# A fused attention and two-layer mixture kernel in two token passes, with Strassen's products in the first layer too

## The chip, the cores and the metric

The kernel runs on one core of a Trainium2 chip. The metric is the device time of one execution in microseconds (us). The core's engines are TensorE (PE, with its weight loads as PEld), VectorE (DVE), ScalarE (ACT), GpSimd (POOL) and SyncE (SP), which issues the DMAs.

## The reference: what is computed

Attention within chunks of 64 tokens (4 batches, 8 heads, 576 tokens, head size 64) gives x of 2304 tokens x 512. Layer 1 is a gated product, layer 2 a mixture of four experts:

```python
scores = (q_c @ k_c.T) / sqrt(64); attn = softmax(scores); x = (attn @ v_c) as (2304, 512)
x = ((x @ w_a) * (x @ w_b)) @ w_out                # w_a, w_b: 512 x 1536, float64; w_out: 1536 x 512
p = domain_probs / (domain_probs.sum(-1) + 1e-9)   # 2304 x 4
out = sum over e of p[:, e] * (relu(x @ w1[e]) @ w2[e])   # w1: 512 x 1024, w2: 1024 x 512
```

## The kernel before

Tokens lie in 18 tiles of 128, grouped in five blocks: block 0 has two tiles, blocks 1 to 4 have four (512 columns in a matmul). Every float32 operand of a large product is split in a high part in fp32r (a cast on ACT, `split_hi`, L90) and a low part (a subtraction on GpSimd or VectorE), and a product is three matmuls: high x low, high x high, low x high (`mm3`, `half_mm`).

The order of the work is written out by hand: lists of small steps (closures) are called one after the other, and each engine runs what it is given in that order. There is one DMA queue, SP's.

**Start.** q, k and v of a tile are loaded (k into a tile `kbd` with zeros beside it, so that two heads are one product), then `emit_S` (scores, PE), `emit_A` (maximum and subtraction, DVE, L218 and L220), `emit_exp` (ACT), `emit_B` (sum and reciprocal on DVE, product on GpSimd, L235), `emit_T` (transposition on PE, copy on ACT) and `emit_V` (PE; ACT casts the high part of x, DVE subtracts the low part, L282). After four tiles, `attn_slot` does one stage of each for successive tiles, between the matmuls of layer 1's first f chunk.

**Layer 1** goes over 12 f chunks of 128, and for each over all five blocks: `moe1_steps` makes the products with w_a and w_b (4 x 3 matmuls each), ACT copies the first, DVE multiplies by the second (L348), the result is split (L90, L352), and one block later `x2_steps` multiplies by w_out (4 x 3 matmuls) and DVE adds into the accumulator `xacc` (L382). Weights come as 512 KB of float64 per piece; `from_f64` turns the two words into float32 with four instructions on DVE (L126 to L132), one on ACT and an integer addition on GpSimd (L142), and `split_w` splits the piece (low part on GpSimd, L149).

**End of layer 1.** `combos` forms, from the accumulators of blocks 1 and 2, the quarter sums of Strassen's algorithm in Winograd's form (B11, B21, T1 to T4, B22), each split (L408, L411).

**Layer 2** goes twice over 16 g (pairs of f chunks of the experts): the first pass p = 0 has blocks 1, 2 and 0, the second blocks 3 and 4. `w_steps` prepares a g: the weights' sums S1 to S4 on GpSimd and six splits. `emit_h_pair` makes the hidden layer of two blocks with 7 products of half depth (6 matmuls each) instead of 8, `emit_h0` block 0's plainly, and `o_tiles` multiplies by w2 and adds p times the result into `oacc` (L582). PSUM is one pool of eight 2 KB buffers.

## Time and profile before

| | |
|---|---|
| median of 3 runs | 1275.64 us (1275.56 to 1276.01) |
| profiled execution, its own time | 1275.81 us |
| its span, first to last instruction | 1273.8 us |
| TensorE busy | 1253.6 us (98%), 6626 instructions |
| VectorE busy | 731.5 us (57%) |
| GpSimd busy | 550.9 us (43%) |
| ScalarE busy | 378.2 us (30%) |
| DMA | 72.43 MB |

Busy shares are means over the span; TensorE's matmuls overlap in the records, so a busy TensorE is not one at its peak. The time outside the span is 2.0 us.

### The profile page before, as it was taken

How to read it: one execution, taken by the hardware profiler on the slowest of the kernel's cores; microseconds unless marked ns; L12 is line 12 of the kernel's file. 1: busy time of each engine (PE TensorE's matmuls, PEld its weight loads, DVE VectorE, ACT ScalarE, POOL GpSimd, SP SyncE). 2: the span in 40 equal slices, each digit the busy share in tenths (PEclk: the TensorE clock that was granted, in tenths of full speed). 3: DMA queues.
4: the chain of work that ended last, by engine and by line, in shares of the span. 5: the costliest groups of instructions: out<-in, count | busy, mean ns of one | idle time of the engine just before them, and what ended most of it. 6: DMA issues, size and time to landing. Idle time of an engine off the chain costs nothing.

```text
span 1273.8 us, 16939 instructions
## 1 busy us (share of the span) xinstructions
PE 1253.6 (98%) x6626; PEld 1048.0 (82%) x6628; DVE 731.5 (57%) x1161; ACT 378.2 (30%) x675; POOL 550.9 (43%) x493
## 2 busy tenths in 40 slices
PE   7899999999999999899999999999999999999998
PEld 5788888888888888688888888888888888888887
DVE  7863555565555555656566555555565556555555
ACT  3554222222222222432332222322232332333231
POOL 4432334343333435455444434344345455554542
PEclk9999999999999999899999999999999999999999
DMA  8731111111111110011110111111131111111111
GB/s 275 223 102 29 38 34 50 50 50 34 49 34 33 50 50 1 33 34 36 48 50 34 34 50 39 45 34 50 33 133 40 60 50 50 51 49 66 34 50 67
DMA packets 25279, 72.43 MB, mean 57 GB/s; under 512 B 3184, under 2 KB 3184, under 8 KB 25200
## 3 DMA queue, kind: packets, MB, share of 16 engines
q1 hardware_dynamic: 25200, 71.35, 17.7%
q8 instruction: 52, 0.85, 0.3%
q14 instruction: 27, 0.22, 0.1%
HBM read 66.62 MB, written 4.72 MB: 56 GB/s over the span
## 4 chain that ended last, share of the span: by engine, by line
PE 92%; DVE 5%; POOL 1%; issue 1%; ACT 1%; DMA 0%; SPq 0%; DVEq 0%; POOLq 0%
PE ps L595 31%; PE ps L479 24%; PE ps L318 12%; PE ps L319 12%; PE ps L320 12%; PE ps L269 1%; DVE d L220 1%; DVE sm L231 1%; DVE mx L218 1%; DVE xl L282 0%; DVE cv L126 0%; DVE sm L232 0%; PE ps L204 0%; POOL cB L408 0%; DMA kbd<-in_k_dram 0%
## 5 line engine op out<-in xcount | busy, mean ns | idle before, releaser
L149 POOL TENSOR_TENSOR wl<-raw,wh 128x512 fp32r<-128x512 f32 x128 | 166.3, 1299 | 340.0 <-ACT wh L90 340.0
L582 DVE SCALAR_TENSOR_TENSOR oacc<-ps,pr,oacc 128x512 f32<-128x512 f32 x270 | 192.5, 750 | 141.4 <-PE ps L595 141.4
L595 PE MATMUL ps<-wl,hh 128*128 128x512 f32 x576 | 224.3, 389 | 0.0
L595 PE MATMUL ps<-wh,hh 128*128 128x512 f32 x576 | 224.2, 389 | 0.0
L595 PE MATMUL ps<-wh,hl 128*128 128x512 f32 x576 | 224.1, 389 | 0.0
L318 PE MATMUL ps<-xl,wh 128*128 128x512 f32 (+1 forms) x488 | 179.7, 368 | 2.3 <-DVE xl L282 1.8
L319 PE MATMUL ps<-xh,wh 128*128 128x512 f32 (+1 forms) x488 | 178.1, 365 | 0.0
L320 PE MATMUL ps<-xh,wl 128*128 128x512 f32 (+1 forms) x488 | 178.0, 365 | 0.0
L479 PE MATMUL ps<-cT,wh 128*128 128x512 f32 x512 | 157.6, 389 | 0.0
L348 DVE TENSOR_TENSOR asb<-ps,asb 128x512 f32<-128x512 f32 (+1 forms) x61 | 38.4, 630 | 191.4 <-PE ps L320 158.5
L352 POOL TENSOR_TENSOR gl<-asb,gh 128x512 fp32r<-128x512 f32 (+1 forms) x61 | 73.2, 1200 | 171.9 <-ACT gh L90 171.9
L382 DVE TENSOR_TENSOR xacc<-ps,xacc 128x512 f32<-128x512 f32 (+1 forms) x220 | 132.3, 633 | 4.0 <-PE ps L320 4.0
L595 PEld LDWEIGHTS ps<-wh,hl 128*128 128x128 f32 x576 | 108.1, 188 | 22.6
L595 PEld LDWEIGHTS ps<-wl,hh 128*128 128x128 f32 x576 | 108.2, 188 | 22.1
L595 PEld LDWEIGHTS ps<-wh,hh 128*128 128x128 f32 x576 | 108.2, 188 | 21.8
L479 PE MATMUL ps<-cB,wh 128*128 128x512 f32 x384 | 118.2, 389 | 0.0
L479 PEld LDWEIGHTS ps<-cT,wh 128*128 128x128 f32 x512 | 96.1, 188 | 20.0
L318 PEld LDWEIGHTS ps<-xl,wh 128*128 128x128 f32 x488 | 92.0, 188 | 18.5 <-DVE xl L282 2.6
L320 PEld LDWEIGHTS ps<-xh,wl 128*128 128x128 f32 x488 | 92.0, 188 | 14.9
L319 PEld LDWEIGHTS ps<-xh,wh 128*128 128x128 f32 x488 | 92.1, 189 | 14.4
L149 POOL TENSOR_TENSOR wl<-s,wh 128x512 fp32r<-128x512 f32 x64 | 83.2, 1299 | 47.2 <-ACT wh L90 47.2
L479 PE MATMUL ps<-cT,wl 128*128 128x512 f32 x256 | 99.6, 389 | 0.0
(85 smaller groups left out, 1962.6 us busy)
## 6 DMA issues: line engine op xcount, KB each, us to landing
raw<-in_w2p_dram SPq DMA_DIRECT2D x64, 512.0 KB, 3.5
raw<-in_w1p_dram SPq DMA_DIRECT2D x36, 512.0 KB, 3.6
q<-in_q_dram SPq DMA_DIRECT2D x18, 256.0 KB, 4.7
kbd<-in_k_dram SPq DMA_DIRECT2D x36, 128.0 KB, 5.2
v<-in_v_dram SPq DMA_DIRECT2D x18, 256.0 KB, 3.3
out_dram<-oacc SPq DMA_DIRECT2D x18, 256.0 KB, 2.0
pr<-in_probs_dram SPq DMA_DIRECT2D x1, 36.0 KB, 5.2
```

The costliest lines, as they stand in the source:

```text
L149: nc.gpsimd.tensor_tensor(out=lo, in0=r, in1=hi.bitcast(F32), op=ALU.subtract)
L218: nc.vector.tensor_reduce(out=mx, in_=ps, axis=AX.X, op=ALU.max)
L220: nc.vector.tensor_tensor(out=d, in0=ps, in1=mx.to_broadcast([P, H, CH]), op=ALU.subtract)
L318: nc.tensor.matmul(out=ps[:, :n], lhsT=wh, rhs=al, start=(m == 0), stop=False)
L319: nc.tensor.matmul(out=ps[:, :n], lhsT=wh, rhs=ah, start=False, stop=False)
L320: nc.tensor.matmul(out=ps[:, :n], lhsT=wl, rhs=ah, start=False, stop=(m == last))
L348: nc.vector.tensor_tensor(out=g[:, :n], in0=st[1][:, :n], in1=g[:, :n], op=ALU.mult)
L352: nc.gpsimd.tensor_tensor(out=gl[:, :n], in0=g[:, :n], in1=gh[:, :n].bitcast(F32), op=ALU.subtract)
L382: nc.vector.tensor_tensor(out=ac, in0=ps[:, :n], in1=ac, op=ALU.add)
L479: nc.tensor.matmul(out=ps, lhsT=x, rhs=y, start=first and kk == 0 and m == 0, stop=kk == 1 and m == 2, skip_group_check=not first,)
L582: nc.vector.scalar_tensor_tensor(out=o, in0=ps, scalar=p1, in1=o, op0=ALU.mult, op1=ALU.add)
L595: nc.tensor.matmul(out=ps[k], lhsT=x[:, s], rhs=y, start=f == 0 and m == 0, stop=f == 1 and m == 2,)
```

## The change

Layer 1 too is done in two token passes, the first over blocks 0, 1 and 2, the second over 3 and 4. Its f chunks are taken in six pairs F. Pair 0 is plain in the first pass (in the attention's place); pairs 1 to 5 of the first pass and all six of the second make the products of two blocks with w_a and w_b by the seven half-depth products that layer 2 already used (`seq`, `seq_a`, `seq_b`); block 0 stays plain (`block0`). `x2_steps` adds both chunks of a pair in one PSUM group. Attention of tiles 13 to 17 moves into the first pass's pairs 1 to 4.

The first pass writes each prepared weight tile (high and low part, 128 x 1024 float32) to DRAM (`entry`, `save`); the second reads it back (`fetch`), and one ACT copy makes it fp32r. The pieces of pair 0 are converted again at the end of the second pass. Layer 2 does the same between its passes. The weights' sums are on DVE (`w_sums`). `from_f64` works in place in the loaded tile. The keys lose their zeros: `emit_S` has 16 products over 64 rows in two PSUM buffers, and `emit_A` four instructions for two. PSUM is two pools of four buffers. The sums over blocks 1 and 2 for layer 2 are formed within the second pass of layer 1, its subtractions on GpSimd.

```diff
+    w_p = ctx.enter_context(tc.tile_pool(name="w", bufs=8))
...
+    ps_p = ctx.enter_context(tc.tile_pool(name="ps", bufs=4, space=bass.MemoryType.PSUM))
+    psm_p = ctx.enter_context(tc.tile_pool(name="psm", bufs=4, space=bass.MemoryType.PSUM))
...
+    def save(behind=0):
+        while len(unsaved) > behind:
+            key, t = unsaved.pop(0)
+            saved[key] = tc.dram_tile([P, 2, 512], F32, name="kept" + "_".join(map(str, key)))
+            nc.sync.dma_start(out=saved[key], in_=t.bitcast(F32))
...
+    def fetch():
+        key = to_fetch.pop(0)
+        save()
...
+        nc.sync.dma_start(out=r, in_=saved[key])
+        fetched[key] = r
...
+    def entry(w, key, names, src, keep):
+        if src is None:
+            t = w_tile()
+            nc.scalar.copy(out=t, in_=fetched.pop(key))
+            if to_fetch and to_fetch[0][0] == key[0]:
+                fetch()
+        else:
+            t = split_w(src)
+            if keep:
+                unsaved.append((key, t))
+                save(2)
...
+    def w_sums(a11, a12, a21, a22):
...
+        add(s1, a21, a22)
+        add(s3, a11, a21, ALU.subtract)
+        add(s2, s1, a11, ALU.subtract)
+        add(s4, a12, s2, ALU.subtract)
...
+    def conv(F, i):
+        key = (0, 2 * F + i % 2, i // 2)
+        f32s[F, i] = from_f64(raws[key].pop(0))
...
+    def seq(w, t, on):
...
+        pa = psum_m()
+        half_mm(pa, w("A11"), c["B11"])
+        nc.scalar.copy(out=t["m1"], in_=pa)
+        yield
+        pb = psum_m()
+        half_mm(pb, w("S2"), c["T2"])
+        add(t["u2"], pb, t["m1"])
+        yield
+        half_mm(pa, w("A12"), c["B21"], first=False)
+        out("11", pa)
+        yield
...
+    def seq_b(F):
...
+        def on(name, ap):
+            g = ga[name]
+            add(g, ap, g, ALU.mult)
+            gh[name], gl[name] = gh_tile(name), ag_tile(F32R)
+            to_parts(g, gh[name], gl[name])
...
+    def x2_steps(F, j, first, last):
...
+            ws = [tuple(x[:, s] for x in wts[0, F][f]) for f in range(2)]
+            mm3(ps, [(*ws[f], *gp[f]) for f in range(2)], n)
...
+        for F in range(1, NP1):
...
+            units = steps_of(seq_a(F, t), 7) + [lambda f=f: block0(F, 0, f) for f in range(2)]
+            units += steps_of(seq_b(F), 7) + [lambda f=f: block0(F, 1, f) for f in range(2)]
...
+            x2p = x2_steps(F, 1, False, last) + x2_steps(F, 2, False, last)
...
+            units += x2p + [lambda i=i: (x20[i](), x20[i + 1]()) for i in (0, 2)]
...
+            put(1, lambda: ent(F, 5, True))
+            put(2, lambda: conv(F, 4))
+            put(3, lambda: ent(F, 6, True))
+            put(5, lambda: (ent(F, 7, True), load_w()))
+            put(6, lambda: conv(F, 5))
...
+                put(10, lambda: conv(nF, 0))
+                put(12, lambda: ent(nF, 0, True))
+                put(14, lambda: conv(nF, 1))
+                put(17, lambda: (sums(nF, 0), load_w()))
+                put(18, lambda: conv(nF, 2))
...
+        order = (*range(1, NP1), 0)
...
+            sa = steps_of(seq_a(F, t), 7)
+            units = sa[:2] + x2
+            units += [lambda: (temps(), sa[2]())] + sa[3:] + steps_of(seq_b(F), 7)
```

`put(u, go)` lets `go` be called ahead of unit u; `conv` and `ent` call `from_f64` and `entry` for piece i or entry n of a pair, `sums` calls `w_sums`.

## Rows read from the trace of the kernel before

**Rows 1.** The page: the share of the chain that ended last by engine, and the busy time and instructions of each engine:

```profile
PE 1253.6 (98%) x6626; PEld 1048.0 (82%) x6628; DVE 731.5 (57%) x1161; ACT 378.2 (30%) x675; POOL 550.9 (43%) x493
...
PE 92%; DVE 5%; POOL 1%; issue 1%; ACT 1%; DMA 0%; SPq 0%; DVEq 0%; POOLq 0%
```

**Rows 2.** Busy time of each engine in two stretches, layer 1 after the attention and the end of layer 1: the stretch and its length, busy us and instructions by engine, granted clock, share of the DMA engines, GB/s:

```profile
101.30:484.00 382.70, 382.70 (x1856) 323.94 (x1857) 207.70 (x367) 95.48 (x172) 138.23 (x111) 1.00 0.14 42
516.70:530.20 13.50, 8.33 (x38) 7.14 (x38) 10.72 (x14) 4.26 (x6) 5.17 (x4) 0.75 0.12 39
```

**Rows 3.** The chain that ended last in order of time, pieces of layer 2: start us, length us, what. L479 is the hidden products of two blocks, L595 those with w2; between a piece of L479 and the next of L595 lie block 0's 24 matmuls of 256 columns, off the chain:

```profile
565.78 13.63 PE ps L595 x60
579.40 9.52 PE ps L479 x42
591.80 13.63 PE ps L595 x60
...
953.20 10.88 PE ps L595 x48
```

**Rows 4.** The timeline of TensorE at the end of layer 1: start us, recorded duration us, engine, line, shapes, count, and in brackets the idle time before and what ended it. 24 matmuls of 256 columns start from the first row up to the second; 12 of 512 columns from the fourth up to the fifth:

```profile
495.88 0.28 PE L318 MATMUL ps<-xl,wh 128*128 128x256 f32 x1
...
498.75 0.40 PE L318 MATMUL ps<-gl,wh 128*128 128x512 f32 x1
...
516.34 0.39 PE L320 MATMUL ps<-gh,wl 128*128 128x512 f32 x1
521.90 0.79 PE L318 MATMUL ps<-gl,wh 128*128 128x512 f32 x1 [5.17 <-POOL gl L352]
...
527.18 0.30 PE L318 MATMUL ps<-yl,wh 128*128 128x256 f32 x1
```

**Rows 5.** The timeline of TensorE in the attention, one slot (scores, transposition, attention x v, layer 1), and the first 512-column chunk:

```profile
31.41 1.09 PE L204 MATMUL ps<-kbd,q 128*64 128x128 f32 x16
32.44 0.66 PE L241 MATMUL ps<-ident,d 128*128 128x128 f32 x4
33.02 1.15 PE L269 MATMUL ps<-aT,v 64*64 64x64 f32 x32
34.10 0.39 PE L318 MATMUL ps<-xl,wh 128*128 128x256 f32 x1
...
72.31 0.50 PE L318 MATMUL ps<-xl,wh 128*128 128x512 f32 x1
```

**Rows 6.** The timeline of VectorE in an attention slot (sum of exponentials, low half of x, maximum, subtraction, first instruction of a conversion):

```profile
42.97 0.69 DVE L231 TENSOR_REDUCE sm<-d 128x8 f32<-128x512 f32 x1 [0.37 <-ACT d L225]
...
44.02 0.64 DVE L282 TENSOR_TENSOR xl<-ps,xh 128x512 fp32r<-128x512 f32 x1
44.57 0.68 DVE L218 TENSOR_REDUCE mx<-ps 128x8 f32<-128x512 f32 x1
45.36 0.69 DVE L220 TENSOR_TENSOR d<-ps,mx 128x512 f32<-128x512 f32 x1
45.96 1.31 DVE L126 TENSOR_SCALAR cv<-raw 128x512 f32<-128x512 f32 x1
```

**Rows 7.** The timeline of VectorE at the end of layer 1: subtractions of two SBUF operands, 1024 wide:

```profile
504.01 2.19 DVE L411 TENSOR_TENSOR xacc<-xacc,xacc 128x1024 f32<-128x1024 f32 x1
506.24 1.65 DVE L411 TENSOR_TENSOR xacc<-xacc 128x1024 f32<-128x1024 f32 x1
...
517.76 1.21 DVE L411 TENSOR_TENSOR xacc<-xacc,xacc 128x1024 f32<-128x1024 f32 x1
```

**Rows 8.** The timeline of GpSimd at the same places (the attention's product; low halves of the sums and of a product):

```profile
45.95 1.05 POOL L235 TENSOR_TENSOR d<-d,rc 128x512 f32<-128x512 f32 x1
...
500.35 4.78 POOL L408 TENSOR_TENSOR cB<-xacc,cB 128x1024 fp32r<-128x1024 f32 x2
505.08 1.72 POOL L352 TENSOR_TENSOR gl<-asb,gh 128x256 fp32r<-128x256 f32 x1
```

**Rows 9.** The timeline of VectorE in the middle of layer 1: four additions from PSUM of 512 columns, the four instructions of a conversion, four additions of 256 columns:

```profile
202.71 2.48 DVE L382 TENSOR_TENSOR xacc<-ps,xacc 128x512 f32<-128x512 f32 x4
205.10 0.42 DVE L126 TENSOR_SCALAR cv<-raw 128x512 f32<-128x512 f32 x1
205.55 0.43 DVE L129 TENSOR_SCALAR cv<-cv 128x512 f32<-128x512 f32 x1
205.89 0.42 DVE L131 TENSOR_SCALAR sg<-raw 128x512 uint32<-128x512 uint32 x1
206.35 0.69 DVE L132 SCALAR_TENSOR_TENSOR cv<-cv,sg 128x512 uint32<-128x512 uint32 x1
...
232.52 1.41 DVE L382 TENSOR_TENSOR xacc<-ps,xacc 128x256 f32<-128x256 f32 x4
```

**Rows 10.** Groups of instructions with their shapes kept apart: line, engine, operation, names, shapes, count | busy us, mean ns | idle before. Low halves of weights and of the sums, 1024 wide:

```profile
L149 POOL TENSOR_TENSOR wl<-raw,wh 128x512 fp32r<-128x512 f32 x128 | 166.3, 1299 | 340.0 <-ACT wh L90 340.0
...
L408 POOL TENSOR_TENSOR cB<-xacc,cB 128x1024 fp32r<-128x1024 f32 x4 | 9.6, 2402 | 0.0
```

**Rows 11.** The page: the DMA queue (packets, MB, share of 16 engines' time over the span), and two kinds of transfer (count, KB each, median us from issue to landing):

```profile
q1 hardware_dynamic: 25200, 71.35, 17.7%
...
raw<-in_w1p_dram SPq DMA_DIRECT2D x36, 512.0 KB, 3.6
...
out_dram<-oacc SPq DMA_DIRECT2D x18, 256.0 KB, 2.0
```

More of the change, by code (lines that the diff above doesn't have):

```diff
@@ L86, in fused_kernel, with sub_hi, add @@
     prs = const.tile([P, NT, 1], F32, name="prs")
[L87 removed]
     def split_hi(dst, src):
         nc.scalar.copy(out=dst, in_=src)
+    def sub_hi(eng, dst, src, hi):
+        eng.tensor_tensor(out=dst, in0=src, in1=hi.bitcast(F32), op=ALU.subtract)
+    def add(out, in0, in1, op=ALU.add):
+        nc.vector.tensor_tensor(out=out, in0=in0, in1=in1, op=op)
     def keep_warm(n):
@@ new lines, in fused_kernel @@
+    fetched = {}
+    to_fetch = [(0, F, n) for F in range(1, NP1) for n in range(10)]
+    to_fetch += [(1, g, n) for g in range(NG2) for n in range(6)]
+    def fetch():
+        key = to_fetch.pop(0)
+        save()
+        if key[0] == 0:
+            tag = "h" + NAMES[key[2] % 4]
+            r = late["p"].tile([P, 2, 512], F32, tag=tag, name="kept")
+        else:
+            r = raw_p.tile([P, 2, 512], F32, tag="raw", name="kept")
+        nc.sync.dma_start(out=r, in_=saved[key])
+        fetched[key] = r
@@ L473, in half_mm, with quarters, in_place, in_turn @@
+    def quarters(x1, x2):
+        return [[x[:, i : i + 2, :]] for x in (x1, x2) for i in (0, 2)]
+    def in_place(x1, x2):
+        q = quarters(x1, x2)
+        return combos(*q, (q[0], q[1], q[2], q[2]))
+    def in_turn(c):
+        s1, s2, s3 = c["sums"]
+        return c["first"] + s1 + c["T3"] + s2 + c["T2"] + s3 + c["T1"] + c["T4"] + c["B22"]
     def half_mm(ps, w, b, first=True):
@@ new lines, in fused_kernel, with block0 @@
+    g0 = {}
+    def block0(F, m, f):
+        if m == 0 and f == 0:
+            g0["a"] = g_p.tile([P, 2, B0], F32, tag="a0", name="a0")
+        w = wts[0, F]
+        ps = psum()
+        ws = []
+        for kk in range(KD):
+            name = (("A11", "A12"), ("A21", "A22"))[f][kk // 2]
+            ws.append(tuple(x[:, kk % 2 * P : kk % 2 * P + P] for x in w[m, name]))
+        h, l = xp[0][0]
+        mm3(ps, [(*ws[kk], h[:, kk, :], l[:, kk, :]) for kk in range(KD)], B0)
+        a = g0["a"][:, f, :]
+        if m == 0:
+            nc.scalar.copy(out=a, in_=ps[:, :B0])
+        else:
+            add(a, ps[:, :B0], a, ALU.mult)
+            if f == 1:
+                for n in "hl":
+                    g0[n] = g_p.tile([P, 2, B0], F32R, tag=f"g{n}0", name=f"g{n}0")
+                to_parts(g0["a"], g0["h"], g0["l"])
@@ new lines, in fused_kernel, with seq_h, on, low @@
+    hs = {}
+    def seq_h(g):
+        tiles = [late["p"].tile([P, 512], F32, tag=n, name=n, bufs=2) for n in ("m1", "u2", "u3")]
+        t = dict(zip(("m1", "u2", "u3"), tiles))
+        t["c22"], t["c12"] = t["m1"], t["u2"]
+        def on(name, src):
+            h = late["p"].tile([P, 2, 512], F32R, tag=f"h{name}", name="h")
+            hh, hl = h[:, 0, :], h[:, 1, :]
+            nc.scalar.activation(out=hh, in_=src, func=ACTF.Relu)
+            hs[name] = (hh, hl)
+            def low():
+                nc.vector.scalar_tensor_tensor(
+                    out=hl, in0=src, scalar=0.0, in1=hh.bitcast(F32), op0=ALU.max, op1=ALU.subtract
+                )
+            return low
+        return seq(lambda x: wts[1, g][x], t, on)
@@ new lines, in fused_kernel @@
+        wait = 0
+        for r, (f, j, i0, nt) in enumerate(spans):
+            steps = list(moe1_steps(f, j, i0, nt, ("12", "21", "11", "22")[r % 4])) + x2
+            x2 = list(x2_plain(f, j, i0, nt))
+            slots = 0
+            if r < 3:
+                _, j1, i1, n1 = spans[r + 1]
+                slots = blocks[j1][0] + i1 + n1 + 3 - slot_no[0]
+            else:
+                x_lo_rest()
+            if r == 3:
+                ca = in_place(qx[1], qx[2])
+                ca_t1 = ca["T1"]
+                s1, s2, s3 = ca["sums"]
+                side = s1 + ca["T3"] + s2 + ca["T2"] + s3 + ca["T4"]
+            done = 0
+            for i, step in enumerate(steps):
+                while done < slots and done * len(steps) <= i * slots:
+                    attn_slot()
+                    done += 1
+                step()
+                if done == slots:
+                    x_lo_rest()
+                if side:
+                    side.pop(0)()
+                if r > 3 and conv_1 and i % 2:
+                    conv_1.pop(0)()
+            if r == 3:
+                domain_probs()
+            while r == 4 and side:
+                side.pop(0)()
@@ L739, in fused_kernel @@
+                if p == 0 and g == 1:
+                    t8 = [ag_tile(F32) for _ in NAMES] + [gh_tile(n, F32) for n in NAMES]
+                    q = quarters(acc[3], acc[4])
+                    cb = combos(*q, [t8[i : i + 2] for i in (0, 2, 4, 6)])
+                    for x in cb["sums"]:
+                        side += x
                 if p == 0 and g == NG2 - 1:
-                    side = side + c_rest
+                    for _ in range(3):
+                        fetch()
+                    b = cb["first"]
+                    side += b[:2] + cb["T2"] + b[2:] + cb["T3"] + cb["T1"] + cb["T4"] + cb["B22"]
```

751 lines of the change are left out of this document (440 added, 311 removed).

## The prediction

> **What bounds the kernel now.** I read the page's chain first: nine tenths of the chain that ended last is TensorE's matmuls, and VectorE's one twentieth lies nearly all in the attention at the start [rows 1]. The busy time by stretch says the same for layer 1: TensorE is busy in all of 101.3 to 484.0 us at full clock, VectorE for 207.7 of 382.7 us and GpSimd for 138.2 [rows 2]. So from 101 us on the time is the number of matmuls by their spacing, and other engines count only where they stop TensorE. The chain in order of time gives the spacing: 42 matmuls of 512 columns in 9.52 us and 48 in 10.88 us, 0.2267 us each [rows 3]. For 256 columns, 24 matmuls start between 495.88 and 498.75 us, 0.12 us each [rows 4]. (Their recorded durations overlap, and are not the cost.) The one pause after the start is at the end of layer 1: TensorE waits 5.17 us for a low half on GpSimd, and the 12 matmuls behind it start over 5.28 us, where 12 x 0.2267 = 2.7 are due [rows 4]; the granted clock of that stretch is 0.75, so part of it ran at 1.2 instead of 2.4 GHz [rows 2].
>
> **Matmuls.** Before, a pair of f chunks over the 8 tiles of two blocks costs 2 f x 2 products x 12 matmuls x 2 blocks = 96 matmuls of 512 columns. After, seq_a and seq_b take 7 products x 6 = 42 each, 84 in all. The w_out products stay (48 per pair and pass). Pairs 1 to 5 save 12 in the first pass, all six in the second: 11 x 12 = 132 matmuls x 0.2267 = **-29.9 us**. Block 0 is plain, in 256 columns, before and after. Layer 2's products are the same in number.
> The row here is 226.7 ns for 512 columns. The Trainium skill's page "TensorE: Matmul & The Clock Gate" (section "Wait — 56ns, not 53.3ns?") gives 215.7 ns warm, for bf16; by that the saving would be 28.5 us, an estimate from the page; the trace decides for this type.
>
> **End of layer 1.** The 5.17 us and the slow matmuls (5.28 - 2.72) go, 7.7 us, if nothing is late in their place. After the change the sums over blocks 1 and 2 are formed while the second pass still works on blocks 3 and 4, and eight w_out steps (48 x 0.2267 = 10.9 us) and block 0's 24 small matmuls lie between the last product and the first that needs them; the remaining splits are 4 ACT casts and 2 lows on each of VectorE and GpSimd, at most 2.4 us each [rows 10]. I take **-7.7 us**.
>
> **Attention on TensorE.** emit_S turns from 8 products of 128 rows into 16 of 64 rows, the shape of emit_V: 32 records in 1.08 us in place of 16 in 1.03 [rows 5], 18 x 0.05 = **+0.9 us**. Memsets (GpSimd, at the start) and the padded keys cost nothing either way.
>
> **Front.** Up to the first 512-column chunk at 72.31 us [rows 5] VectorE is the chain. Per tile the maximum and subtraction took 1.39 us (44.57 to 45.96) and the low half 0.55 [rows 6]; as pairs of 256-column instructions I take 1.6 and 0.68, from 0.34 a piece [rows 9] plus the gap behind a reduction: +0.35 for each of 9 slots, 3 us. One slot of slack before block 2 goes too, so the last low half is waited for (about 2 us); two key loads fewer per tile give back about 1. **+4 us**, bounds 0 and +8. The attention of tiles 13 to 17 moves into the first pass, under more matmuls, at equal TensorE cost.
>
> **Preparing weights, first pass.** This is the tight place. Take pair 2. TensorE: 132 x 0.2267 + 72 x 0.12 = 38.6 us, and two attention slots of 1.08 + 0.58 + 1.08 [rows 5], 44.1 in all. VectorE: six conversions of four instructions, 205.10 to 206.96 us = 1.86 each, 11.2; eight half-width sums of 0.34, 2.7 (they were GpSimd's in layer 2); 22 PSUM reads of 0.61 and 6 of 0.34, 15.4 [rows 9]; two slots of 1.05 + 1.6, 5.3 [rows 6]. That is 34.6 of 44.1: it fits alone. GpSimd: 6 integer adds, 10 low halves of weights, 5 of products, 21 x 1.30 = 27.3 [rows 10], and two attention products of 1.05 [rows 8]: 29.4.
> But the two do not run freely beside each other. A conversion's first instruction takes 0.42 us alone [rows 9], and 1.31 where a GpSimd product of 1.05 us began at the same moment (45.95 and 45.96 us) [rows 6, 8]. The subtraction of two SBUF operands takes 1.21 us alone and 2.19 behind GpSimd's low halves, and GpSimd's 256-wide low half then takes 1.72 until the subtraction ends [rows 7, 8]. PSUM reads show no such wait. So conversions and sums (11.2 + 2.7) and all of GpSimd's 29.4 want the same thing in turn: 43.3 of 44.1 us. Pairs 3 and 4 stand no better (41.8 of 43, 40.3 of 41.4).
> The stretch ahead of it is worse: block 2 with f = 0 to block 2 with f = 1 is 27.6 us of matmuls, with four 1024-wide subtractions and two lows at 1.2 [rows 7], four conversions and eight sums on VectorE (17.3), and on GpSimd four adds, five lows of weights, the products' lows and one 1024-wide low at 2.4 [rows 10] (18.7): 36.0 in 27.6. With pair 1 it makes 80.5 us in 74.3, so 6 at least; I take 8, as x in the combos also waits on casts in turn. For pairs 2 to 4 an order made by program order will not use 97% without waits; with four PSUM buffers a kind, each filled in 6 x 0.2267 = 1.36 us, VectorE may be some 4 us late before TensorE stops. I take 2.3 us each, 7. Bounds: 0, and 8 each (below).
> Second pass: pairs 1 to 4 need ten 1024-wide ACT casts and no GpSimd low for weights; free. The last two pairs carry conversions again and GpSimd's four wide subtractions: 64 us in turn in 59.8 of matmuls, with the w_out tail behind: +3. Layer 2's first pass moves the sums to VectorE (+1.4 us per g, where GpSimd is idle), its second drops GpSimd's lows for six casts: nothing. Stalls together **+18 us**, bounds +2 and +46.
>
> **DMA.** Kept weights are 146 tiles of 0.524 MB written and read. The queue moved 71.35 MB in 17.7% of the span, 316 GB/s while busy [rows 11]. In pair 2: 6 raw + 10 kept pieces and two tiles of attention, 10 MB, 31.5 us of 44. Loads have 7 units (9 us) from issue to use, against 3.6 us to landing [rows 11]; a save is issued two entries late, so SP rarely waits with loads behind it. I cost it at nothing; if writes took twice their share, 48 us would be wanted in 44.
>
> **Sum.** -29.9 - 7.7 + 0.9 + 4 + 18 = -14.7 on the span of 1273.8: 1259.1, and with the 2.0 us around it (1275.81 against 1273.8) **1261 us**. The profiled run stands 0.2 us over the median of 1275.64.
>
> **Rivals.**
> 1. Covered (30 in 100): the units place each low half between two conversions, so the turns rarely collide, and stalls stay under 10 us: 1241 to 1253, at best -29.9 - 7.7 + 0.9 + 2 = 1241. For it: pairs in layer 1 before show single waits only. Against: 43.3 of 44.1.
> 2. Taking turns sets the pace, slower (14 in 100): if a GpSimd instruction is always ready when VectorE starts one that wants the turn, each such instruction waits up to 1.3 us. With some 16 such waits a pair, VectorE has 34.6 + 21 = 55 us; I take 8 us over 44.1 for pairs 1 to 4, 8 ahead of them and 6 in the second pass, 46 in all: 1276 - 36.7 + 4 + 46 = **1289**. It decides against the change from 33 us of stalls on, about 6 a pair.
> The Trainium skill's page "SBUF — State Buffer" (section "Who interferes with whom") states this rule: one port pair, held for a whole instruction by whichever came first, wanted by all of GpSimd and by VectorE with two SBUF inputs or in a two-port mode. The rows of 504 to 507 us agree.
> 3. DMA (6 in 100): kept tiles delay raw ones; 4 to 5 us for each of 5 pairs: about 1280. Against it: an output of 256 KB lands in 2.0 us [rows 11], so writes are not slow.
> A remainder of 5 in 100 ends between.
>
> **How the numbers follow.** Forecast as summed: 45 in 100, own range 1253 to 1273. Low bound 1244 leaves out the best of rival 1; high 1281 leaves out rival 2. A time within 0.2% (2.6 us of 1275.6) can't be told from no change. Faster by more: 45 + 30, with a little off, 75; same 6; slower 19.
>
> **What would show it.** In the profile after: 132 fewer 512-column matmuls; no pause before layer 2; clock full after the start; in the first pass (about 75 to 300 us) conversions of VectorE well over 0.42 us beside GpSimd's low halves, TensorE waiting for VectorE or for a gl of GpSimd. It would be wrong if layer 1's first pass shows no waits (nearer 1245), if pairs take 50 us and more (slower), or if waits name a DMA.

## The result and the profile after

The changed kernel takes 1292.09 us (median of 4 runs, 1291.12 to 1294.23) against 1275.6: a ratio of 1.0131, interval 1.0113 to 1.0148. It is slower by 16.5 us, where 14.7 us less were forecast. The profiled execution took 1291.12 us with a span of 1289.2. The page after: the engines (busy us, share, instructions), the shares of the chain that ended last, the DMA queue, and the two transfers of kept tiles (count, KB each, us to landing):

```profile
PE 1236.6 (96%) x6782; PEld 1027.2 (80%) x6784; DVE 858.5 (67%) x1354; ACT 494.4 (38%) x776; POOL 392.0 (30%) x302
...
PE 83%; DVE 13%; ACT 1%; issue 1%; DMA 0%; POOL 0%; SPq 0%; DVEq 0%; ACTq 0%; POOLq 0%
...
q1 hardware_dynamic: 63216, 210.83, 48.0%
...
kept<-w SPq DMA_DIRECT2D x146, 512.0 KB, 5.4
kept<-kept SPq DMA_DIRECT2D x146, 512.0 KB, 4.5
```

Beside [rows 1], TensorE is busy for 17 us less and the kernel is longer all the same: VectorE's share of the chain goes from 5% to 13%. The DMA's share of it rounds to 0%, with three times the bytes of [rows 11].

The chain in order of time, the seven-product work of layer 1's second pass and the first of layer 2 (start us, length us), and last the first of layer 2 in the kernel before:

```profile
380.31 19.04 PE pm L597 x84
410.23 19.04 PE pm L597 x84
...
470.07 13.62 PE pm L597 x60
...
545.09 9.52 PE pm L597 x42
```

```profile
530.24 9.55 PE ps L479 x42
```

In the second pass a pair comes every 29.92 us (410.23 - 380.31). That is (84 + 48) x 0.2267, nothing lost: the forecast saving is there. From 470 us on it isn't. Layer 2 starts at 545.09 us, 14.9 us later than before (530.24), and from there the two kernels take equally long, within 0.6 us. So the loss lies in layer 1. It begins earlier than before (70.62 us, [rows 5]: 72.31); its matmuls, taken from the forecast's own terms, are 530.24 - 72.31 - 29.9 - 7.7 + 0.9 = 421 us, and it takes 545.09 - 70.62 = 474.5: 53 us of waits and of slow clock where 18 were put. A count of the matmuls and attention slots of the trace from 70.62 us on, at the forecast's spacings and the slot's measured times, gives the same 421 us.

Where they lie. TensorE's timeline, the first product of the work that stopped (start us, recorded us, idle us before it and its releaser):

```profile
92.56 0.39 PE L453 MATMUL ps<-ag,w 128*128 128x256 f32 x1 [1.84 <-POOL ag L95]
...
104.63 0.50 PE L453 MATMUL ps<-ag,w 128*128 128x512 f32 x1 [3.38 <-POOL ag L95]
...
150.73 0.79 PE L453 MATMUL ps<-ag,w 128*128 128x512 f32 x1 [3.08 <-DVE a L98]
...
199.96 0.50 PE L453 MATMUL ps<-ag,w 128*128 128x512 f32 x1 [3.09 <-DVE a L98]
...
251.12 0.47 PE L453 MATMUL ps<-ag,w 128*128 128x512 f32 x1 [2.77 <-DVE xacc L98]
...
492.98 0.80 PE L453 MATMUL ps<-ag,w 128*128 128x512 f32 x1 [3.19 <-POOL ag L95]
...
528.15 1.95 PE L597 MATMUL pm<-cB,w 128*128 128x512 f32 x6 [3.96 <-DVE gh L98]
```

Two stages show these: the first pass, about once a pair, and the last two pairs of the second. The pauses of over 0.3 us sum to 32 of the 53 us; the rest is in shorter waits and in the clock. By stretch (up to unit 7 of pair 1, from unit 7 of one pair of the first pass to unit 7 of the next, then four stretches of the second pass; busy us of TensorE, its weight loads, VectorE, ScalarE, GpSimd; granted clock, DMA share, GB/s):

```profile
70.62:126.11 55.49, 48.38 (x266) 38.95 (x267) 47.01 (x69) 22.43 (x41) 24.63 (x19) 0.91 0.36 120
126.11:175.44 49.33, 45.69 (x341) 38.32 (x340) 42.54 (x75) 17.83 (x32) 28.66 (x23) 0.97 0.57 188
175.44:223.77 48.33, 44.53 (x341) 37.32 (x340) 42.81 (x75) 17.82 (x32) 28.84 (x23) 1.00 0.57 188
223.77:270.87 47.10, 42.96 (x277) 36.12 (x276) 40.47 (x64) 16.90 (x30) 27.38 (x22) 1.00 0.54 176
270.87:314.74 43.87, 41.96 (x238) 35.47 (x236) 38.87 (x60) 15.19 (x27) 25.76 (x21) 0.96 0.58 192
...
380.00:410.00 30.00, 30.00 (x134) 24.86 (x133) 14.65 (x21) 14.64 (x19) 5.94 (x4) 1.00 0.51 175
470.00:500.00 30.00, 26.81 (x107) 21.66 (x106) 22.40 (x29) 11.49 (x18) 22.73 (x15) 0.89 0.11 36
500.00:545.00 45.00, 38.52 (x172) 31.50 (x172) 36.34 (x49) 17.07 (x26) 28.31 (x18) 0.96 0.32 105
470.07:545.09 75.02, 65.35 (x278) 53.17 (x277) 58.66 (x77) 28.50 (x44) 51.04 (x32) 0.93 0.24 77
```

VectorE is busy for 42.81 of 48.33 us, where before it had 207.7 of 382.7 [rows 2]. In the stretch of 380 to 410 us, with kept weights and no conversion, it is busy for 14.65 of 30.00 us and nothing stops.

VectorE's timeline in pair 2, from the end of the second forms to the second multiplication into `a`, which reads block 0's PSUM buffer and so frees it (TensorE's wait names it `DVE a`):

```profile
187.62 0.43 DVE L140 TENSOR_SCALAR raw<-raw 128x512 f32<-128x512 f32 x1
188.09 1.48 DVE L143 TENSOR_SCALAR raw<-raw 128x512 f32<-128x512 f32 x1
...
190.92 1.09 DVE L98 TENSOR_TENSOR ag<-gh,ag 128x512 f32<-128x512 f32 x1
...
192.65 0.69 DVE L98 TENSOR_TENSOR ag<-gh,ag 128x512 f32<-128x512 f32 x1
193.25 0.42 DVE L98 TENSOR_TENSOR a<-ps,a 128x256 f32<-128x256 f32 x1
193.59 2.61 DVE L98 TENSOR_TENSOR s<-raw 128x256 f32<-128x256 f32 x2
...
196.91 0.68 DVE L345 TENSOR_REDUCE sm<-d 128x8 f32<-128x512 f32 x1
...
199.49 0.41 DVE L98 TENSOR_TENSOR a<-ps,a 128x256 f32<-128x256 f32 x1
```

and GpSimd's beside it:

```profile
187.98 1.30 POOL L95 TENSOR_TENSOR ag<-ag,gh 128x512 fp32r<-128x512 f32 x1 [1.35 <-ACT gh L92]
190.42 1.04 POOL L152 TENSOR_TENSOR raw<-raw 128x512 int32<-128x512 int32 x1 [1.15 <-issue]
192.81 3.11 POOL L95 TENSOR_TENSOR ag<-ag,gh 128x512 fp32r<-128x512 f32 x2 [1.34 <-ACT gh L92]
```

The turns of the forecast are here: the clamp L143 takes 1.48 us beside a low half of 1.30 (L140, the same form ahead of it, 0.43 alone), and two sums of 256 columns take 2.61 us beside two low halves. A product's multiplication of two SBUF operands takes 1.09 us where GpSimd's integer addition is under way as it begins and 0.69 where no GpSimd instruction is. Behind the sums comes the attention slot, and only behind that the multiplication that frees block 0's buffer. From 187 to 199.9 us VectorE has no gap, and TensorE has stood since 196.9.

### The profile page after: what moved, and what is told of

It reads as the page before. It is cut to its first block, busy times and chain, and to the rows that moved or that the text cites. A ratio compares the mean times of both kernels' runs of the same rounds, so it can differ in the third digit from the quotient of the medians.

```text
span 1289.2 us, 17904 instructions
## 1 busy us (share of the span) xinstructions
PE 1236.6 (96%) x6782; PEld 1027.2 (80%) x6784; DVE 858.5 (67%) x1354; ACT 494.4 (38%) x776; POOL 392.0 (30%) x302
## 4 chain that ended last, share of the span: by engine, by line
PE 83%; DVE 13%; ACT 1%; issue 1%; DMA 0%; POOL 0%; SPq 0%; DVEq 0%; ACTq 0%; POOLq 0%
PE pm L597 38%; PE ps L821 30%; PE ps L453 5%; PE ps L454 5%; PE ps L455 5%; DVE ag L98 2%; DVE s L98 2%; DVE raw L140 1%; DVE raw L143 1%; DVE raw L144 1%; DVE gh L98 1%; DVE d L332 1%; DVE sg L136 1%; DVE mx L331 1%; DVE x L556 1%
## 5 line engine op out<-in xcount | busy, mean ns | idle before, releaser
L821 PE MATMUL ps<-w,h 128*128 128x512 f32 x1536 | 353.3, 389 | 0.0
L821 PEld LDWEIGHTS ps<-w,h 128*128 128x128 f32 x1536 | 288.3, 188 | 59.9
L597 PE MATMUL pm<-cT,w 128*128 128x512 f32 x1296 | 312.7, 390 | 0.0
L597 PEld LDWEIGHTS pm<-cT,w 128*128 128x128 f32 x1296 | 243.2, 188 | 50.9
L597 PE MATMUL pm<-cB,w 128*128 128x512 f32 x972 | 247.4, 392 | 5.2 <-DVE gh L98 4.0
L597 PEld LDWEIGHTS pm<-cB,w 128*128 128x128 f32 x972 | 181.6, 189 | 42.8 <-DVE gh L98 4.4
L95 POOL TENSOR_TENSOR w<-raw,w 128x512 fp32r<-128x512 f32 x106 | 141.0, 1332 | 223.4 <-ACT w L92 147.4
L196 ACT CAST w<-kept 128x1024 fp32r<-128x1024 f32 x146 | 148.6, 1046 | 61.5 <-DMA kept<-kept 38.1
L453 PE MATMUL ps<-ag,w 128*128 128x512 f32 (+1 forms) x204 | 83.4, 409 | 31.0 <-POOL ag L95 12.1
L454 PE MATMUL ps<-gh,w 128*128 128x512 f32 (+1 forms) x244 | 91.8, 376 | 0.0
L455 PE MATMUL ps<-gh,w 128*128 128x512 f32 (+1 forms) x244 | 91.7, 376 | 0.0
L453 PEld LDWEIGHTS ps<-ag,w 128*128 128x128 f32 x204 | 40.0, 196 | 46.3 <-POOL ag L95 14.9
L152 POOL TENSOR_TENSOR raw<-raw 128x512 int32<-128x512 int32 x42 | 44.1, 1049 | 79.7 <-PE ps L455 23.6
```

The costliest lines, as they stand in the source:

```text
L95: eng.tensor_tensor(out=dst, in0=src, in1=hi.bitcast(F32), op=ALU.subtract)
L152: nc.gpsimd.tensor_tensor(out=high.bitcast(I32), in0=high.bitcast(I32), in1=low.bitcast(I32), op=ALU.add)
L196: nc.scalar.copy(out=t, in_=fetched.pop(key))
L453: nc.tensor.matmul(out=ps[:, :n], lhsT=wh, rhs=al, start=(m == 0), stop=False)
L454: nc.tensor.matmul(out=ps[:, :n], lhsT=wh, rhs=ah, start=False, stop=False)
L455: nc.tensor.matmul(out=ps[:, :n], lhsT=wl, rhs=ah, start=False, stop=(m == last))
```

## The experiments

A pair means here the time from unit 7 of one pair of the first pass to unit 7 of the next: 49.3, 48.3, 47.1 and 43.9 us in the changed kernel. Single runs compare with 1292.1; its own four runs spread over 3 us, so differences under 2 us are none, and one of 3 us alone shows little. Part of the spread is the clock: the run with the first other order (below) is the changed kernel up to unit 17 of pair 1, yet it reaches unit 7 of that pair at 123.78 and not 126.11 us, and its granted clock in 70.62 to 126.11 us is 0.97, not 0.91.

**Fewer turns: the ten low halves of weights of a pair from GpSimd to ScalarE.**

```diff
+            if key[0] == 0 and key[1] > 0:
+                t = w_tile()
+                split_hi(t[:, 0, :], src)
+                split_hi(t[:, 1, :], src)
```

> The low halves of layer 1's weights in the first pass are ACT casts of the source instead of GpSimd subtractions, so the low part of w_a, w_b and w_out is wrong and that part of the computation is left out; ten GpSimd instructions of 1.3 us fewer in each of pairs 1 to 5, VectorE's own work unchanged, ACT 6 us more per pair. Turns between GpSimd and VectorE set the pace: pair 2 falls from 48.3 us to 45 or less, the span by about 20 us to 1270. VectorE's own amount or the order of its queue sets it: pair 2 stays at 47 to 48.5 and the span within 6 us of 1289.

1289.54 us; pairs 49.0, 48.9, 48.0, 43.2. The stretch of pair 2, and its pause, with the first matmul of 256 columns behind the 36 of 512 that follow the pause; then that matmul in the changed kernel, whose 36 began at 199.96 us:

```profile
172.43:221.35 48.92, 45.80 (x342) 38.43 (x340) 39.43 (x75) 22.93 (x42) 15.64 (x13) 0.97 0.54 184
```

```profile
196.53 0.80 PE L458 MATMUL ps<-ag,w 128*128 128x512 f32 x1 [3.09 <-DVE a L98]
...
206.41 0.28 PE L458 MATMUL ps<-gl,w 128*128 128x256 f32 x1
```

```profile
208.30 0.28 PE L453 MATMUL ps<-gl,w 128*128 128x256 f32 x1
```

GpSimd lost 13 of 28.8 us and VectorE 3.4 of its 42.8, and the pause is as long as it was. What VectorE waits for in that place are mostly the products' low halves, which stayed. So fewer turns elsewhere in the pair don't shorten this pause. The pair's length says less than it seems to: behind the same pause the 36 matmuls took 9.88 us here and 8.34 in the changed kernel, as the first seven ran at the lower clock. Without these 1.5 us pair 2 would be 0.9 us shorter than there, not 0.6 longer.

**Less on VectorE: the accumulations of pairs 1 to 5's w_out products as ScalarE copies** (`if first or j < 3`).

> The first pass's w_out products of pairs 1 to 5 are copied out of PSUM by ACT instead of added by VectorE, so the accumulation over pairs is left out there; VectorE has ten PSUM reads (6.2 us) less per pair, none of which ever waited for GpSimd, and the conversions, sums and GpSimd's work are as before. VectorE's amount sets the pace: pair 2 falls to 45 or less and the span by about 20 us. Turns set it: pair 2 stays at 47 or more, since the same conversions and sums collide with the same low halves ahead of block 0's multiplication.

1291.06 us; pairs 49.4, 50.6, 44.5, 42.1, pauses of 3.08 and 3.07 us on `a` as before. Pairs 3 and 4 gain 2.6 and 1.8 us, pair 1 nothing, and pair 2 is 2.3 us longer: the accumulations come behind the pause. Here too the clock hides a part. Pair 2's pause and the first matmul of 256 columns behind its 36 of 512:

```profile
198.55 0.79 PE L453 MATMUL ps<-ag,w 128*128 128x512 f32 x1 [3.07 <-DVE a L98]
...
209.68 0.28 PE L453 MATMUL ps<-gl,w 128*128 128x256 f32 x1
```

These 36 took 11.13 us, 2.8 more than in the changed kernel, so at equal clock pair 2 would gain about 0.5 us. And of the 7 us taken from VectorE (8 x 0.69 + 4 x 0.38) its busy time in pair 2 shows 2.6, 40.20 for 42.81: other instructions take longer (the clamp L143 0.93 us in the mean for 0.77, the first instruction L136 0.71 for 0.50), as waits for turns do.

**Order: the sums behind block 0 (unit 17 to 18), the next conversion 18 to 20, the second attention slot 17 to 22.**

> Same work, other places in pairs 1 to 4: the sums of the next pair one unit later (behind block 0's multiplication), the conversion of piece 2 at unit 20, the second attention slot at unit 22. If the wait of 3.1 us a pair is only the order (a PSUM buffer held by block 0's product behind the sums and the slot), it goes: 3 us a pair, the span near 1278. If VectorE lacks the time for the pair's work, waits included, the wait reappears at a later w_out product and the span stays within 4 us of 1289.

1291.9 us; pairs 49.3, 48.9, 46.5, 44.9. The wait has a new name and the same length:

```profile
192.10 0.79 PE L453 MATMUL ps<-ag,w 128*128 128x512 f32 x1 [2.92 <-POOL ag L95]
```

Now it is the low half of the third product: its multiplication stands behind the conversion at unit 14 (184.69 to 187.87 us on VectorE, with 1.47 us for L143), and the low half follows over ScalarE and GpSimd.

**Buffers: five PSUM buffers for single products, three for the seven forms** (`bufs=5`, `bufs=3`).

> Only the PSUM pools change: five buffers for the small products and w_out, three for the seven-product sequences, instead of four and four. If the split of PSUM is what turns VectorE's delay into TensorE's, one buffer more is worth one w_out product (1.4 us) a pair: about -7 us over the first pass. If VectorE's delay per pair is more than the buffers can hold at all, at most 2 us in all, or a loss where the sequences wait for their third buffer.

1284.04 us. In pairs 1 and 2 the pauses on `a` are 0.93 us, and others come, of 1.21 us on the scores' buffers and 0.9 on an accumulation, all on VectorE; pairs 3 and 4 have some of 1.2 to 1.8. VectorE is as busy as ever, 43.85 us of 47.9 in pair 2.

**Order again: the conversion of unit 14 too goes behind the forms** (14 to 17, the sums to 19, the third conversion to 21, the slot to 22).

> Order alone: of the work that VectorE does for the next pair while the fourth form's second half runs, the conversion of the second w_b piece goes behind that half (unit 14 to 17), the sums from 17 to 19, the conversion of the third piece from 18 to 21, the second attention slot from 17 to 22. Nothing is left out. Theory 'burst' (a backlog of some 9 us in VectorE's in-order queue at the end of the second form's products makes the pause of 3 us a pair): the pauses at the w_out products of pairs 1 and 2 fall from 3.1 us to under 1, those pairs from 49.3 and 48.3 us to 46-47, the kernel from 1292 to 1283-1286 us. Theory 'full' (VectorE has 42 us of work and turns in a pair of 43, so the same backlog shows up elsewhere): pairs stay at 48-49, 1290-1292 us.

1292.76 us; pairs 49.0, 48.9, 46.5, 43.5. The pause of 3.1 us became four:

```profile
198.32 1.15 PE L391 MATMUL ps<-aT,v 64*64 64x64 f32 x32 [1.08 <-DVE xacc L98]
201.82 0.50 PE L453 MATMUL ps<-ag,w 128*128 128x512 f32 x1 [0.76 <-DVE xacc L98]
206.05 0.50 PE L453 MATMUL ps<-ag,w 128*128 128x512 f32 x1 [1.17 <-DVE xacc L98]
210.30 0.39 PE L453 MATMUL ps<-gl,w 128*128 128x256 f32 x1 [1.18 <-DVE xacc L98]
```

Together 4.2 us: the accumulations of the w_out products now wait behind what was moved. The theory of one bad place falls here.

**The way to pair 1, the second pass's end, and sums on GpSimd, each alone.** The first moves `domain_probs` to the second pass and takes pair 1's first weights at every third step; the second moves the y sums (the sums over blocks 1 and 2 for layer 2) to other units of the last two pairs and leaves three of six steps that prepare y for after the last products; the third gives the weights' sums of pairs 2 to 5 to GpSimd. Its expectation names pair 0 as well, but its code (`nc.gpsimd if F > 1`) leaves that pair's sums on VectorE; the trace has them there.

> Two edits between the end of the attention stage and pair 1: domain_probs (four VectorE instructions, 3.6 us there) moves to the start of the second pass, and the eleven pieces of pair 1's first weights are taken at every third step, not every second. Nothing is left out. Theory 'burst': the multiplication of the plain products stands 5 us behind conversions that come two in a row; the pauses of 1.8, 1.1, 3.4 and 0.8 us between 92 and 108 us fall to 2 in all, pair 1 starts 5 us earlier, 1286-1288 us. Theory 'full': the conversions are late instead, pair 1 starts as before and 1291 us stays.

1288.84 us, between the two expectations: unit 7 of pair 1 comes 3 us earlier, but the first other order reached it 2.3 us earlier without this edit. The pauses of 1.8 and 1.1 us at 93 and 95 us are gone; that of 3.4 us at the last plain product stays.

> The end of the second pass alone: the four y sums on GpSimd (2.4 to 2.6 us each) go from beside the second forms of the last two pairs to where no low half of a product is due (units 12 and 13 of pair 5, units 2 and 7 of pair 0), and only three of six steps that prepare y go ahead of the last products. Nothing is left out. Theory 'burst': the pauses of 3.2 us at 493 and 4.0 at 528 go, and with them the two stretches at 0.86 and 0.93 of the clock; layer 2 starts 7-11 us earlier, 1281-1285 us. Theory 'full' (the last two pairs have too much for GpSimd and VectorE wherever it stands): 1290-1292 us.

1289.26 us. The pauses at 493 and 528 us are gone; 1.2, 2.8, 1.7, 0.5, 0.7, 0.9 and 1.0 us have come between 498 and 542.

> The four weight sums of each half of pairs 2 to 5 and pair 0 are made by GpSimd, not VectorE (order as in the changed kernel). Nothing is left out. It takes 4 to 5 us of a pair, turns counted, from VectorE, 3.3 of it in the backlog ahead of the release of block 0's PSUM buffer, and gives GpSimd about as much, ahead of the products' low halves. Theory 'burst': the pause on that release goes, and a shorter one on the low halves may come in its place; pairs 46-47 us, 1283-1287 us. Theory 'full' gives the same here. Rival 'turns' (it is the number of instructions on both engines that share turns, whichever engine has them): pairs stay 48-49, 1290-1294 us.

1288.96 us, again between the expectations; pairs 47.5, 47.4, 47.9, 43.9; at the place of the pause on `a` 1.1 us are left, on an accumulation, and one of 1.3 us is new.

**The second pass's end with less work in it**: three conversions and a set of sums from pair 5 back to pair 3, two low halves from GpSimd to VectorE.

> The second pass alone. What VectorE does for pair 0's weights (three conversions, the first half's sums) goes from pair 5 to pair 3, which has room; two of pair 0's low halves go from GpSimd to VectorE; the y sums stand at units 11 and 12 of pair 5 and 6 and 9 of pair 0; two of six steps that prepare y go ahead of the last products. Nothing is left out. Theory 'load' (the last two pairs are short of VectorE and GpSimd time together, so that moving work inside them, as tried, only moves the pauses): some 9 us of VectorE's work leave pair 5, the pauses after 470 us fall from 9.7 us to under 4, layer 2 starts 7-11 us earlier, 1281-1284 us. Rival 'chain' (it is the last chain of multiplication, copy and low half that the products wait for, whatever the load): the pauses at 528 and 493 us stay and it is 1288-1291 us.

1287.45 us: layer 2 starts at 541.54 us, 3.5 earlier, half of the least that was expected. The pauses at 493 and 528 us are gone; the longest left is one of 3.38 us at 513.7, on a form's sum of VectorE.

**Less on VectorE in the conversions: the scaling to ScalarE, two clamps as one instruction.**

```diff
+        nc.scalar.activation(out=t, in_=t, func=ACTF.Copy, scale=H_SCALE)
...
+        nc.vector.tensor_scalar(
+            out=t, in0=t, scalar1=H_MAX, scalar2=-H_MAX, op0=ALU.min, op1=ALU.max
+        )
```

> One edit: in each conversion of a float64 piece from pair 1's fifth on, the scaling goes to ScalarE (38% busy), two units ahead, and VectorE's two clamps become one instruction: three VectorE instructions for four, and none that runs on VectorE while it waits for ScalarE. Nothing is left out. Theory 'load' (VectorE with its turns has 42-43 us of work in a pair of 43.2): 4-5 us of a pair go, pairs 1 to 4 fall from 49.3, 48.3, 47.1 and 43.9 us to 45-47, 1281-1285 us. Theory 'burst' (only what stands ahead of one release counts): the conversion in the backlog shortens from 3.1 to about 2 us, the pause by 1 us a pair, 1286-1288 us. Rival 'turns of the products' low halves alone': no change, 1290-1292 us.

1284.8 us; pairs 48.7, 47.2, 47.7, 42.6. The time is what 'load' expected, the pairs are not: they give 2.4 of the 7.3 us, and 3.1 are gained ahead of unit 7 of pair 1, with a granted clock of 0.97 for 0.91 in 70.62 to 126.11 us.

**No conversion on VectorE at all for pairs 2 to 5.** Everything else, its order too, stays.

> VectorE's four instructions of each conversion are left out for pairs 2 to 5 in the first pass (those weights are then wrong); ScalarE's and GpSimd's part, the order and everything else stay. Theory 'load': 12 us with their turns leave each pair's 42 us of VectorE, so pairs 1 to 4 fall from 49.3, 48.3, 47.1 and 43.9 us to 43-45 and the pauses to under 1 us a pair, 1272-1277 us. Theory 'buffer' (the pause on block 0's PSUM buffer comes from the sums and the attention slot that stand ahead of it, 6 us, whatever the load): pauses of 1.5-3 us a pair stay, 1280-1285 us.

1277.21 us; pairs 45.7, 45.6, 42.1, 39.9. The stretches of pairs 2 to 4:

```profile
171.54:217.14 45.60, 43.93 (x341) 37.29 (x340) 27.78 (x50) 17.61 (x32) 28.31 (x23) 1.00 0.59 194
217.14:259.24 42.10, 42.10 (x278) 36.30 (x276) 23.75 (x39) 16.70 (x30) 28.28 (x23) 1.00 0.59 199
259.24:299.12 39.88, 39.88 (x237) 34.47 (x236) 22.85 (x36) 15.04 (x27) 26.22 (x21) 1.00 0.62 208
```

The pause that is left in pair 2:

```profile
193.89 0.50 PE L457 MATMUL ps<-ag,w 128*128 128x512 f32 x1 [1.67 <-DVE a L98]
```

This shows where most of the first pass's loss comes from. With 15 us less on VectorE in a pair, and GpSimd as busy as before, pairs 3 and 4 have TensorE busy throughout: 42.1 and 39.9 us is what their matmuls take, and the changed kernel lost 5.0 and 4.0 us on them. In pairs 1 and 2 one pause of 1.7 us on `a` is left, behind the sums and the slot; the rest went with the conversions. The run takes away VectorE's load and what stands ahead of its multiplications at once, so by itself it doesn't tell one from the other. That two later orders gave nothing speaks for load; that pairs 1 and 2 gained under 1 us, clock counted, where VectorE had 2.6 to 3.4 us less to do elsewhere, speaks for the place.

**All edits together** (buffers, `domain_probs`, sums on GpSimd, scaling on ScalarE, the second pass's end), in the old order and in the later one:

> All edits together, in the changed kernel's own order: five PSUM buffers for single products and three for the forms, domain_probs and pair 1's first weights moved, sums of weights on GpSimd, scaling on ScalarE, and the second pass's end as in the run for that. Nothing is left out. Theory 'load': the effects add, as VectorE comes down to about 34 us of a pair: pairs of 44-45 us, 1258-1266 us, under the kernel before. Theory 'chain' (the latency from the last product over VectorE, ScalarE and GpSimd to the w_out products sets the pair once the buffers do not): pairs of 46, 1268-1275 us.

1277.43 us, slower than either expectation; pairs 49.1, 46.9, 45.8, 43.6.

> The same with the later order of the second conversion, the sums, the third conversion and the second attention slot (units 17, 19, 21 and 22). Nothing is left out. Theory 'load': the order makes no difference once VectorE has room, within 2 us of the run with the old order. Theory 'chain': the conversion that stood ahead of the last multiplications is gone, the pause at the w_out products too, and this run is 3-6 us faster than that one, 1258-1265 us.

1280.47 us: the later order is 3 us slower, not faster (single runs both). The gains don't add: alone, the five edits of the first run gave 8.1, 3.3, 3.1, 7.3 and 4.6 us, 26 together, and it gave 14.7.

**Rearranged from that trace**, once with the sums on GpSimd, once on VectorE, and once on VectorE with four and four buffers:

> All edits together again, with the places mended where the trace of that run shows ScalarE waiting for a DMA ahead of the first form's copy (the scaling of a piece is put behind the time at which it lands), the sums and second slot behind block 0, pair 1's first weights not beside the last plain product, and the y sums of pair 0 side by side. Sums of weights on GpSimd, five and three PSUM buffers. Nothing is left out. 'Load': 1266-1272 us.

> As the run before, with the sums of weights on VectorE. 'Load' (4 to 5 us a pair more for VectorE): 4-8 us slower than with the sums on GpSimd. 'Turns' (GpSimd at 36 of 50 us makes more of VectorE's SBUF instructions wait, so that the move gives nothing): the same within 2 us.

> As the run before, with the PSUM buffers shared four and four, as in the changed kernel. 'Buffer' (with three buffers the attention scores hold two, and the forms' products wait for VectorE to read them: 1.5 us a pair in the run of all edits): 3-5 us faster than with five and three. 'Load': single products wait for their evictions instead, no gain or 2-4 us slower.

1289.89, 1289.06 and 1284.12 us, ratios to the kernel before 1.0106 (1.0091 to 1.0121), 1.0100 (1.0083 to 1.0117) and 1.0063 (1.0048 to 1.0078). Which engine makes the sums is no matter in this order, as 'turns' expected and 'load' did not. With three buffers the second forms wait 3.0 to 3.5 us for the attention scores, as a conversion now stands just ahead of the slot at unit 5; with four they don't. The run that was to be mended had taken 1277.4, so the first became 12 us slower by moves that were each aimed at a pause of its trace.

**Small moves only**: all edits as in the first such run, with three collisions taken away; and the same with the first slot of a pair at unit 7:

> The first run of all edits together with four places moved and nothing else: the scaling of a pair's fifth and sixth piece one unit later, so that ScalarE does not wait for their DMA ahead of the first form's copy, and in pair 0 the two low halves of VectorE and the last conversion away from the y sums, the last of which goes behind the products. Nothing is left out. 'Place' (what is left are such collisions, each worth its pause): the pauses of 1.7 and 0.6 us at the start of pairs 2 and 3 and of 3.8 us at 504 go, 1268-1272 us. 'Load' (VectorE with its turns is late by then, whatever stands ahead): the pauses come back beside other work, 1275-1278 us.

> As the run before, with the first attention slot of a pair behind the first forms (unit 7, not 5), and pair n+1's first conversion and entry one unit later. Nothing is left out. 'Place': the pauses for the score buffers (1.5 and 0.4 us) at the start of pairs go as well, 1-2 us a pair, 1263-1269 us. 'Load': no gain, within 2 us of the run before; a pause for the score buffers at the second forms takes their place.

1274.5 us, ratio 0.9996 (0.9987 to 1.0005), and 1277.22 us, ratio 1.0016 (1.0006 to 1.0025). The first is 17.6 us faster than the changed kernel and level with the kernel before, which no version here beats; the second is 2.7 us slower, where a gain or a change of under 2 us was expected. Its pair 2:

```profile
170.52:217.30 46.78, 44.54 (x342) 37.78 (x340) 36.89 (x61) 21.16 (x38) 34.83 (x31) 1.00 0.58 187
```

VectorE is down from 42.8 to 36.9 us, GpSimd up from 28.8 to 34.8, and no pause of over 0.8 us is left in it. It is still 46.78 us long, 3.6 us more than pair 2's matmuls and slots as the forecast counts them (38.6 + 2 x 2.3, the scores at 0.63).

## Why the prediction was wrong

**Right.** The matmuls: 29.92 us a pair in the second pass, and TensorE without a pause in pairs 3 and 4 of the run that leaves the conversions out. The DMA: 211 MB cost nothing; kept tiles landed in 5.4 and 4.5 us, and TensorE never waits for one (ScalarE is idle for 38 us ahead of its casts for them, off the chain). The 146 ScalarE casts and the changed layer 2 cost no more than 0.6 us. The pause at the end of layer 1 as it was is gone (another came, below). The order of the stages was right, and so was where to look: conversions beside GpSimd's low halves, TensorE waiting for VectorE or a gl.

**Over-priced.** Front: -1.7 us where +4 was put, though the granted clock there was lower (0.88 in 25 to 75 us, 1.00 before). The two points aren't alike: by its first 512-column chunk the changed kernel has done the scores of 13 tiles, the kernel before of 15, and the forecast counted the later slots as equal. emit_S: 32 records of 64 rows take 0.63 us, not the 1.08 of emit_V's shape; the same 18 slots save 7 us of TensorE's time rather than cost 0.9. What of it reached the end was not measured alone.

**The step that failed is "Stalls together +18".** The mechanism was named, but the term was mis-sized in every stretch: 53 us in its place. Taking the run without conversions as what the matmuls need (with its 1.7 us pauses taken off), pairs 1 to 4 lost 5.4, 4.4, 5.0 and 4.0 us; 2.3 was put for each of pairs 2 to 4. Up to unit 7 of pair 1 it was 13 us (55.49, where 150 matmuls of 512 columns, 48 of 256 and a slot take 42.1), and 8 was put for this and pair 1. The last two pairs of the second pass and the tail lost 15 us (470.07 to 545.09 is 75.0; 252 matmuls of 512 columns and 24 of 256 take 57.1 + 2.9); 3 was put.

Why each was too small:

- The forecast added up turns as a capacity, 43.3 of 44.1 us, and took the 34.6 us of VectorE's own work to "fit alone". A turn that VectorE waits for is VectorE's time as well: its queue is in order, and what stands behind the waiting instruction waits too. 34.6 became 42.8 busy us of a pair whose matmuls and slots need 43.2; by the trace's groups, conversions, sums and multiplications take some 7 us longer in it than alone. So beside one resource at 98% there was VectorE at 99%. That the conversions' part of this counts is shown by the run without them. That the full share as such sets the pace isn't shown: pair 2 had VectorE at 39.4 and 40.2 us in the first two runs and kept its pause.
- The turns themselves were under-counted. Three of a pair's four product multiplications read two SBUF operands and wait for GpSimd like the sums; the forecast had them among the "PSUM reads of 0.61" that don't wait. With them its 43.3 would be about 45, over the 44.1 that it set them against.
- "VectorE may be some 4 us late before TensorE stops" priced the cover by four PSUM buffers. Where it matters the cover is block 0's 2.9 us, the slot and two w_out products (12 matmuls up to 196.9 us in pair 2): from the last forms to the w_out products the chain is VectorE's sum, a multiplication of two SBUF operands (1.1 us beside GpSimd), ScalarE's cast, GpSimd's low half. A conversion there delays it by 3.1 us. Five and three buffers gave 8 us in this order, and cost 5 in the rearranged one; the two moves of order alone gave none.
- At the end of the second pass the four wide subtractions of GpSimd take 2.4 to 2.6 us each, and a VectorE instruction that meets one waits it out (L140 2.39 us at 489.42). They were placed beside the last products' low halves, and the final splits ahead of the last forms' sums. The forecast had summed 64 us of turns in 59.8 and not asked where they fall. That these places cause the 15 us is argued from the trace: moving them (1289.26 us) moved the pauses, and taking work out of these pairs (1287.45) gave 3.5 us.
- The clock was taken as full. In six of the nine rows of stretches above it was granted at 0.89 to 0.97, so part of each ran at 1.2 and not 2.4 GHz. All six hold pauses, but so do pairs 2 and 3, with 1.00: some pauses cost more than their length, as the 8.34, 9.88 and 11.13 us behind pair 2's same pause in three runs show. As an estimate, what the clock falls short of 1 times the length, summed over 70.62 to 175.44, 270.87 to 314.74 and 470.07 to 545.09 us, puts 13 of the 53 us or so at most down to it.

Rival 2 had the right sign and nearly the time (1289) at 14 in 100, and its count of waits was wrong: VectorE's busy time in pair 2 is 8 us over its 34.6, not 21, and a pair lost 4 to 5.4 us where it put 8; the end it put at 6 us was 15. Its sum was near because these offset each other; that was luck. (Rival 3's 1280 us lies more than 2.6 us above the kernel before, so its 6 in 100 belonged to slower and not to same.) The Trainium skill's page "SBUF — State Buffer" (section "Who interferes with whom") states the rule that it rests on, and the trace agrees: 0.43 us alone and 1.48 beside a low half.

What stays open: why the edits' gains don't add. After all of them VectorE has room in a pair (36.9 of 46.8 us), and the loss is spread over waits of 0.3 to 0.8 us and shorter ones. Both a chain of four engines with little slack and GpSimd's 34.8 us of turns fit this; no run takes them apart.

## What to carry to other kernels

Before work is moved under another engine's cover, add each engine's waits for turns to its own time and set this against the stretch it must fit, stage by stage: here an in-order engine that was nearly full came late by whole microseconds at every burst, and moving instructions within it moved the pause. The same pause lowered the clock in some runs and not in others, so compare a stretch's length only with its granted clock beside it. Then follow the one chain that the next stage needs, hop by hop, against the matmuls that cover it. Saved matmuls were worth nothing here in the stretches where the preparing engine was nearly as full as TensorE: four pairs of the second pass kept their whole saving, and the stretches in which VectorE prepares weights gave back more than theirs.

## What the hardware showed unexpectedly

- 64 x 64 products: 32 records in 0.63 us (189.38 to 190.01) in emit_S, whose products take all four pairings of row half and output half, and 1.08 (190.60 to 191.68) in emit_V, which has two of them. That the pairings make the difference was not tried by itself.

```profile
189.38 0.69 PE L320 MATMUL pm<-k,q 64*64 64x64 f32 x32
190.01 0.66 PE L355 MATMUL ps<-ident,d 128*128 128x128 f32 x4
190.60 1.15 PE L391 MATMUL ps<-aT,v 64*64 64x64 f32 x32
191.68 0.39 PE L453 MATMUL ps<-xl,w 128*128 128x256 f32 x1
```

- 512 KB written to DRAM landed in 5.4 us and read back in 4.5 with the queue at 48% of the 16 engines' time, and TensorE never waited for it.
- VectorE's multiplications of two SBUF operands of 512 columns between 110 and 530 us of the changed kernel: the 13 that began with no GpSimd instruction under way took 0.69 us, as with one operand in PSUM; the 19 that began beside one took 1.03 to 2.17.
- The same pause of 3.1 us of TensorE was followed by full clock in one run and by 7 and 14 matmuls at the lower one in two others (36 matmuls in 8.34, 9.88 and 11.13 us).
